# A banded-attention and FFN kernel: the order of all engines' steps read from a complete list instead of made by a list scheduler

## The chip, the core and the metric

One Trainium2 chip, one of its cores. The core has five engines that run side by side and wait for one another through semaphores: TensorE (PE, matmuls), VectorE (DVE), ScalarE (ACT), GpSimd (POOL) and SyncE (SP), which here issues nearly all DMAs. The metric is the device time of one execution in microseconds (us). Three runs of the kernel before took 624.2, 625.16 and 625.16 us; the median is 625.16.

## The reference

```python
# q, k, v: (4, 8, 768, 64); n_global = 8, n_local = 96; w_ch1: (512, 2048), w_ch2: (2048, 512)
scores = q @ k^T / 8                       # per batch and head
keep = (col < n_global) | (0 <= row - col < n_local)
dist = n_local where only global, else |row - col|
scores = where(keep, scores - slope[head] * dist, -1e9)
a = softmax(scores);  attn = a @ v         # divided by sum + 1e-9
x = attn with the heads side by side       # (4, 768, 512)
xn = (x - mean) / sqrt(var + 1e-6) * g_ln
out = x + relu(xn @ w_ch1) @ w_ch2
```

The weights arrive as 64-bit floats, everything else that is large as 32-bit floats.

## The kernel before

**Tiles.** The 3072 rows are 24 tiles of 128 rows, numbered 0 to 23 (`TILES`, line 49). Tiles 0 to 3 are the first tiles of the four batches; they attend to themselves only and are done in float32 (`first`, line 551). Tiles 4 to 23 attend to their own 128 keys, the 128 before, and the global keys; they are done in pairs of float16 high and low parts (`attention`, line 647). Two tiles make a chunk; chunk c holds the tiles 2c and 2c + 1.

**Steps of a tile in `attention`.** k, q and v are loaded (L291) and split into high and low parts on ACT, DVE and POOL (L489, L490, L657, L658, L497, L498). A transposing DMA lays out k (L492) and q (L660), and two plain DMAs copy q's halves across (L662). Four times, for two heads each: PE makes scores (L685, 8 matmuls), DVE adds the mask and takes the minimum (L544), ACT takes the exponential (L549), DVE and POOL split it (L690, L691), a transposing DMA lays it out (L693), and PE multiplies by v (L512 to L514, twelve matmuls, called rows here). Then DVE divides (L524), takes the moments (L531 to L533), POOL takes the root (L536), and DVE scales (L708).

**Steps of a chunk.** In chunks 0 to 3 the first FFN product is plain (L809 to L811 for tiles 0 to 3, L837 to L839 for chunks 2 and 3). From chunk 4 on a pair of tiles is joined in seven products instead of eight (`seven`, line 850): ACT scales (L718), POOL makes three differences (L726 to L729), ACT and DVE split the sums into high and low (L740, L741), transposing DMAs lay them out (L742), and PE makes seven products of 24 matmuls for each of two halves (L862 to L864) with sums taken on ACT and DVE between them (L875, L878). Each result passes through ACT and DVE (L820, L821) into float16 pairs. The second FFN product is 48 matmuls a tile in steps of six (L935; L912 for the last tile, in two halves), DVE adds x (L944, L919), and SP stores the tile (L947, L922).

**Weights.** Sixteen blocks of 1 MB are loaded (L392) and turned from 64-bit floats into float16 pairs by a chain on ACT and DVE: L400, L404, L412, L416, then a copy (L435 or L437) and a difference (L439 or L441).

**What sets the order.** No step is emitted as it is written. `banded` (line 232) records 2165 steps with `Plan.op`: the engine, a duration, what it reads and writes. `Plan.order` (line 141) adds the waits for reused buffers and works out how urgent a step is; `Plan.forward` (line 174) is a list scheduler that keeps a clock of each engine and takes the most urgent step that is ready, with the constants `LOOK` and `EAGER` and the table `SHIFT`, which adds a number to the urgency of each group of steps. Its result, a list of steps with planned start times, is emitted in that order (`emit`), so each engine's program holds its steps in that order and an engine never passes a step that waits.

**Fillers.** Before each PE step that is planned in the first 130 us, `hold` (line 1043) puts matmuls on a tile of zeros (L1047), as many as fill 0.8 of the planned gap. They write into a bank that also holds attention results.

**The end.** When all is done a verdict is summed by one PE step (L1038) and turned into a flag by four small DVE steps (L1027 to L1030). Every engine loads the flag (L1266) and branches past a general version of the kernel that is used for other inputs. The last 40 steps stand in a block of their own (`LAST`).

Of the kernel before, what the change touches and what calls it, by code (L numbers as in the profile page):

```python
# [86 lines left out]
class Plan:  # L87
# [3 lines left out]
    MARGIN = {"DMA": 2.0}  # L91
# [49 lines left out]
    def order(self, chain, stretch, lead):  # L141
        for bufs, made in self.rings.values():
            for old, new in zip(made, made[bufs:]):
                for o in new.users:
# [2 lines left out]
        place = {o: n for n, o in enumerate(self.ops)}
        waits = {o: len(o.before) for o in self.ops}
        line, ready = [], [o for o in self.ops if not waits[o]]
        while ready:  # L150
            o = ready.pop()
            line.append(o)
            for p in o.behind:
                waits[p] -= 1
                if not waits[p]:
                    ready.append(p)
        assert len(line) == len(self.ops), "a circle"
        nxt = dict(zip(chain, chain[1:]))
        rank = {o: n for n, o in enumerate(chain)}
        left = {}  # L160
        for n, o in reversed(list(enumerate(chain))):
            left[o] = o.took * stretch + (left[nxt[o]] if o in nxt else 0.0)
        need = {}
        for o in reversed(line):
            most = left.get(o, 0.0)
            for p in o.behind:
                extra = lead if p in rank and o not in rank else 0.0
                most = max(most, need[p] + o.took + self.seen(o) + extra)
            need[o] = max(most, o.took)
        self.need, self.place = need, place  # L170
        self.planned = self.forward(SHIFT)
        return [o for _, o in self.planned]

    def forward(self, shift):

        need, place = self.need, self.place
        due = {o: need[o] + shift.get(o.group, 0.0) for o in self.ops}
        waits = {o: len(o.before) for o in self.ops}
        engines = ("PE", "ACT", "DVE", "POOL", "SP")
        free = dict.fromkeys(engines, 0.75)  # L180
        dma = port = 0.0
        end, known = {}, {e: [] for e in engines}

        def offer(o):
            t = max([o.after] + [end[p] for p in o.before])
            m = max([t] + [end[p] + self.MARGIN["DMA"] for p in o.before if p.xfer is not None]) if o.engine == "PE" else t
            known[o.engine].append((t, m, -due[o], place[o], o))

        for o in self.ops:
            if not waits[o]:  # L190
                offer(o)
        plan = []
        while any(known.values()):
            best = None
            for e in engines:
                if not known[e]:
                    continue
                can = [(max(c[0], port), max(c[1], port), *c[2:]) if c[4].port else c for c in known[e]]
                at = max(free[e], min(c[0] for c in can))
                now = [c for c in can if c[1] <= at] or [c for c in can if c[0] <= at]  # L200
                c = min(now, key=lambda c: (c[2], c[3]))
                soon = [d for d in can if d[0] <= at + LOOK * c[4].took and d[2] < c[2] - EAGER]
                if soon and e != "PE":
                    c = min(soon, key=lambda c: (c[2], c[3]))
                at = max(free[e], c[0])
                if best is None or at < best[0]:
                    best = (at, e, c[4])
            at, e, o = best
            known[e] = [c for c in known[e] if c[4] is not o]
            free[e] = at + o.took  # L210
# [8 lines left out]
            for p in o.behind:
                waits[p] -= 1  # L220
                if not waits[p]:
                    offer(p)
# [9 lines left out]
def banded(ctx, tc, q, k, v, n_global, n_local, g_ln, w1, w2, out, flag):  # L232
    nc = tc.nc
    vec, act, pool, sp, pe = nc.vector, nc.scalar, nc.gpsimd, nc.sync, nc.tensor
# [153 lines left out]
    def weight(src, dh, dl, name, n, engine="SP", uses=()):  # L388
# [35 lines left out]
        if how[0] == "D":  # L424
            op("DVE", 1.1, lambda: b_(vec), r=[st], w=[lo], port=True)
# [128 lines left out]
    def first(ts):  # L554
# [19 lines left out]
        for e in range(2):  # L574
            for t in ts:
# [457 lines left out]
    op("DVE", 1.42, ranges, r=["cnt", *(("big", n_) for n_ in range(NF))], w=["ok"], after=450.0)  # L1033
# [6 lines left out]
    plan.order(main, 1.13, LEAD)  # L1040
# [43 lines left out]
LEAD = 12.0  # L1084
# [23 lines left out]
SHIFT = {"a0": 820.0, "a1": 286.0, "a2": 108.0, "a3": 701.5, "f0": 21.0, "f1": -345.5, "f10": -235.0, "f2": 34.5, "f5": -15.5, "f7": -246.0, "f8": -72.0, "f9": -54.0, "g": 43.0, "m.a": 196.5, "m.d": -8.5, "s": 31.0, "t0.k": -12.0, "t0.p": 442.5, "t0.s": -26.0, "t0.x": 120.0, "t1.k": -11.0, "t1.p": 823.0, "t1.s": 740.5, "t1.x": 391.0, "t10.s": 127.5, "t10.x": 743.5, "t11.s": -21.0, "t11.x": 722.5, "t12.k": 624.5, "t12.s": 172.0, "t12.x": 431.0, "t13.s": -80.5, "t14.k": -432.0, "t14.s": 318.5, "t15.k": -155.5, "t15.s": 13.0, "t15.x": -67.5, "t16.x": 97.0, "t17.k": -259.0, "t17.s": -134.0, "t18.k": 301.5, "t18.s": 869.0, "t19.x": -379.5, "t2.k": -612.5, "t2.p": 446.0, "t2.s": -18.0, "t2.x": 531.5, "t20.k": -443.5, "t20.s": 33.5, "t21.s": -58.0, "t21.x": 810.5, "t22.k": 600.0, "t22.s": -46.5, "t23.k": -581.0, "t23.s": -220.5, "t3.k": -590.0, "t3.p": 320.0, "t3.s": -371.0, "t3.x": 98.0, "t4.k": -338.0, "t4.s": 227.0, "t4.x": 59.0, "t5.k": 1576.5, "t5.s": 804.0, "t5.x": 1039.0, "t6.k": -664.5, "t6.s": 75.0, "t6.x": 87.5, "t7.k": 211.5, "t7.s": 189.5, "t7.x": 31.0, "t8.k": 80.0, "t8.s": 4.5, "t9.s": -6.5, "t9.x": 495.0, "w1_0_0": -19.0, "w1_0_1": -367.5, "w1_1_0": -7.5, "w1_1_1": -360.0, "w1_2_0": -44.5, "w1_2_1": -300.0, "w1_3_0": 297.0, "w1_3_1": 841.0, "w2_0": -334.5, "w2_1": 76.0, "w2_2": -332.0, "w2_3": 22.5, "w2_4": -548.0, "w2_5": -183.0, "w2_6": -33.5, "w2_7": 16.5, "y10": -235.0, "y2": 34.5, "y4": 12.0, "y5": -15.5, "y7": -246.0, "y8": -72.0, "y9": -54.0}  # L1108
# [191 lines left out]
```

## Time and profile before

| | |
|---|---|
| three runs | 624.2, 625.16, 625.16 us |
| median | 625.16 us |
| profiled execution, first to last instruction | 621.1 us |
| PE busy | 600.4 us (97%), 7036 matmuls, of them 154 fillers |
| DVE busy | 436.9 us (70%) |
| ACT busy | 329.2 us (53%) |
| POOL busy | 246.0 us (40%) |

The page gives the span of the profiled execution, 621.1 us, and no launch-to-end time of that execution; the median of the runs is 4.06 us above the span. PE's busy time counts matmuls that overlap once, counts fillers, and does not tell at which clock they ran. The granted clock is 1.00 in all but one of the forty slices of the page, 0.8 to 0.9 in that one (about 248 to 264 us).

### The profile page before, as it was taken

The page shows a single profiled execution, that of the slowest core. Times are in us where ns is not written, and L with a number is a line of the kernel's source. Part 1 is how long each engine was busy: PE and PEld are TensorE (multiplying, and loading weights), DVE is VectorE, ACT ScalarE, POOL GpSimd, SP SyncE. Part 2 cuts the span into 40 slices and gives each one's busy share as a digit, 9 for nine tenths or more (in the row PEclk, how much of TensorE's full clock was granted, in tenths as well). Part 3 has the DMA queues.
Part 4 walks back from the last instruction along what each step waited for, and adds up shares of the span by engine and source line. Part 5 has one row for each costly group of instructions (what it writes and reads, how often), then busy time and mean ns, then how long its engine had stood idle before and what let it go on. Part 6 is the DMA issues. An engine that isn't in the chain of part 4 may idle for free.

```text
span 621.1 us, 17187 instructions
## 1 busy us (share of the span) xinstructions
PE 600.4 (97%) x7036; PEld 453.3 (73%) x7036; DVE 436.9 (70%) x996; ACT 329.2 (53%) x798; POOL 246.0 (40%) x230
## 2 busy tenths in 40 slices
PE   7889999999999999799999999999999999999996
PEld 5778999555956865596696695787687695796774
DVE  3899898988656474895896995885686784773431
ACT  3887887754535453564564563663663652642220
POOL 1234345448786772434432452441533432323000
PEclk9999999999999999899999999999999999999999
DMA  8996979978485946899697798998997692540301
GB/s 241 308 282 136 250 213 262 174 156 188 72 156 103 174 95 111 176 139 181 117 181 156 162 168 107 188 145 129 170 176 143 136 129 60 111 70 20 77 1 40
DMA packets 260263, 91.65 MB, mean 148 GB/s; under 512 B 250192, under 2 KB 250448, under 8 KB 260176
## 3 DMA queue, kind: packets, MB, share of 16 engines
q1 hardware_dynamic: 259888, 90.47, 74.1%
q8 instruction: 57, 0.93, 0.6%
q14 instruction: 30, 0.25, 0.2%
q10 hardware_dynamic: 288, 0.00, 0.0%
HBM read 38.01 MB, written 6.29 MB: 71 GB/s over the span
## 4 chain that ended last, share of the span: by engine, by line
PE 74%; DVE 13%; ACT 6%; POOL 3%; issue 2%; DMA 1%; ACTq 0%; DVEq 0%; POOLq 0%
PE bank L935 31%; PE bank L862 7%; PE bank L864 7%; PE bank L863 7%; PE bank L685 5%; PE bank L838 2%; PE bank L839 2%; PE bank L837 2%; DVE arena L404 2%; DVE arena L416 2%; PE bank L912 2%; ACT arena L549 2%; PE bank L514 1%; PE bank L512 1%; PE bank L513 1%
## 5 line engine op out<-in xcount | busy, mean ns | idle before, releaser
L935 PE MATMUL bank<-w2h,arena 128*128 128x512 f16 x736 | 239.4, 381 | 0.1
L935 PEld LDWEIGHTS <-arena 128*128 128x128 f16 x1104 | 102.7, 98 | 104.7 <-issue 2.9
L691 POOL TENSOR_TENSOR arena<-arena 128x512 f16<-128x512 f32 x80 | 97.9, 1226 | 182.6 <-DVE arena L690 131.9
L935 PE MATMUL bank<-w2l,arena 128*128 128x512 f16 x368 | 140.1, 381 | 0.1
L862 PE MATMUL bank<-arena 128*128 128x128 f16 x512 | 88.5, 219 | 1.3 <-ACT bank L875 0.9
L863 PE MATMUL bank<-arena 128*128 128x128 f16 x512 | 88.5, 219 | 0.0
L864 PE MATMUL bank<-arena 128*128 128x128 f16 x512 | 88.5, 219 | 0.0
L549 ACT ACTIVATE arena<-arena,mn 128x256 f32<-128x256 f32 x160 | 80.1, 501 | 5.1
L544 DVE CUSTOM_DVE_ANT_0 arena<-bank,mask 128x256 f32<-128x256 f32 x160 | 60.4, 417 | 17.3 <-POOL arena L691 12.6
L862 PE MATMUL bank<-arena,w 128*128 128x128 f16 x384 | 66.6, 219 | 3.3 <-DVE arena L821 3.2
L864 PE MATMUL bank<-arena,w 128*128 128x128 f16 x384 | 66.7, 219 | 0.0
L863 PE MATMUL bank<-arena,w 128*128 128x128 f16 x384 | 66.7, 219 | 0.0
L821 DVE SCALAR_TENSOR_TENSOR arena<-bank,arena 128x512 f16<-128x512 f32 x64 | 43.7, 687 | 31.7 <-ACT arena L820 31.5
L820 ACT ACTIVATE arena<-bank 128x512 f16<-128x512 f32 x64 | 37.8, 592 | 39.3 <-PE bank L864 35.9
L863 PEld LDWEIGHTS <-arena 128*128 128x128 f16 x512 | 50.1, 98 | 3.3 <-issue 1.7
L862 PEld LDWEIGHTS <-arena 128*128 128x128 f16 x512 | 50.1, 98 | 1.7
L864 PEld LDWEIGHTS <-arena 128*128 128x128 f16 x512 | 50.1, 98 | 0.0
L690 DVE CAST arena<-arena 128x512 f16<-128x512 f32 x80 | 43.1, 542 | 8.8 <-DMA arena<-arena 4.4
L685 PE MATMUL bank<-kT,qT 128*128 128x128 f16 x640 | 47.3, 219 | 1.1 <-DVE nm L544 1.0
L685 PEld LDWEIGHTS <-qT 128*128 128x128 f16 x640 | 39.9, 98 | 10.0 <-issue 2.3
L536 POOL TENSOR_TENSOR rs<-rs,half 128x1 f32<-128x1 f32 x24 | 23.4, 975 | 58.4 <-DVE rs L533 58.4
L547 ACT ACTIVATE mn<-nm 128x2 f32<-128x2 f32 x80 | 15.8, 197 | 49.9 <-DVE nm L544 49.1
(181 smaller groups left out, 1499.0 us busy)
## 6 DMA issues: line engine op xcount, KB each, us to landing
arena<-in_moe_w_ch_dram SPq DMA_DIRECT2D x16, 1024.0 KB, 6.8
kf<-in_k_dram SPq DMA_DIRECT2D x28, 256.0 KB, 4.2
vf<-in_v_dram SPq DMA_DIRECT2D x28, 256.0 KB, 4.3
qf<-in_q_dram SPq DMA_DIRECT2D x24, 256.0 KB, 4.0
out_dram<-x SPq DMA_DIRECT2D x23, 256.0 KB, 2.5
qT<-qT SPq DMA_DIRECT2D x40, 128.0 KB, 2.9
pT<-arena SPq DMA_TRANSPOSE x80, 3.2
arena<-arena SPq DMA_TRANSPOSE x36, 3.2
```

Of the source, the lines that this page charges most:

```text
L536: op("POOL", 0.98, lambda: pool.tensor_tensor(out=rs(), in0=rs(), in1=half, op=ALU.pow), r=["half"], w=[rs])
L544: vec.tensor_tensor_reduce(out=T()[:, u, :], in0=ps()[:, u], in1=mask(h), scale=1.0 / Z, scalar=3e38, op0=ALU.add, op1=ALU.min, accum_out= ...
L549: act.activation(out=T()[:, u, :], in_=T()[:, u, :], func=AF.Exp, scale=-1.0, bias=mn()[:, h:h + 1], accum_out=sm()[:, h:h + 1])
L685: pe.matmul(ps()[:, u, n_ * P:(n_ + 1) * P], lhsT=qT()[:, a * H + h, :], rhs=use[n_][0]()[:, h, :], start=(a == 0), stop=(a == 1))
L690: op("DVE", 0.33, lambda pn=pn, T=T: vec.tensor_copy(out=pn()[:, :, 0, :], in_=T()), r=[T], w=[(pn, "hi")], port=True)
L691: op("POOL", 1.2, lambda pn=pn, T=T: pool.tensor_tensor(out=pn()[:, :, 1, :], in0=T(), in1=pn()[:, :, 0, :], op=ALU.subtract), r=[T, (pn, ...
L820: op("ACT", 0.49, lambda: act.activation(out=hh()[:, 0], in_=src(), func=AF.Relu), r=[key], w=[(hh, "hi")])
L821: op("DVE", 0.6, lambda: vec.scalar_tensor_tensor(out=hh()[:, 1], in0=src(), scalar=0.0, in1=hh()[:, 0], op0=ALU.max, op1=ALU.subtract), r ...
L862: pe.matmul(ps()[:, i, :], lhsT=wh, rhs=xT()[:, hi + kk, :], start=(first_ and i == 0 and kk == 0), stop=False, skip_group_check=True)
L863: pe.matmul(ps()[:, i, :], lhsT=wh, rhs=xT()[:, lo + kk, :], start=False, stop=False, skip_group_check=True)
L864: pe.matmul(ps()[:, i, :], lhsT=wl, rhs=xT()[:, hi + kk, :], start=False, stop=(i == 3 and kk == 1), skip_group_check=True)
L935: pe.matmul(ps[t](), lhsT=h[:, part, :], rhs=w[:, f + a, :], start=(f + a == 0 and n_ == 0), stop=(f + a == NF - 1 and n_ == 2))
```

## The change

The list scheduler goes. `Plan.order` takes no arguments: it adds the waits for reused buffers as before and then takes the steps in the order of a table `STEPS` of 2165 numbers, which came from a local search outside the kernel. `Plan.times` replaces `forward`: it gives each step of that list a planned start, which decides only how many fillers go ahead of a PE step and how long DVE and POOL steps are tied to one another (`TIED`). Three recorded durations change (L425 from 1.1 to 1.25, L597 from 1.3 to 1.1, L996 from 1.42 to 0.6); they too have no other effect. What is computed, the buffers and the waits between steps stay the same; no instruction is added or taken away but fillers.

```diff
-    MARGIN = {"DMA": 2.0}
-    def order(self, chain, stretch, lead):
+    def order(self):
         for bufs, made in self.rings.values():
             ...
-        self.need, self.place = need, place
-        self.planned = self.forward(SHIFT)
-        return [o for _, o in self.planned]
-    def forward(self, shift):
-        ...
+        assert sorted(STEPS) == list(range(len(self.ops)))
+        self.planned = self.times([self.ops[n] for n in STEPS])
+
+    def times(self, steps):
+
+        free = dict.fromkeys(("PE", "ACT", "DVE", "POOL", "SP"), 0.75)
+        dma = port = 0.0
+        end, plan = {}, []
+        for o in steps:
+            assert all(p in end for p in o.before), "a step ahead of what it needs"
+            at = max([o.after, free[o.engine]] + [end[p] for p in o.before] + [port] * o.port)
+            free[o.engine] = at + o.took
+            ...
+            plan.append((at, len(plan), o))
+        return [(at, o) for at, _, o in sorted(plan, key=lambda x: x[:2])]
-    plan.order(main, 1.13, LEAD)
+    plan.order()
-SHIFT = {"a0": 820.0, "a1": 286.0, "a2": 108.0, ...}
+STEPS = [
+    3, 2, 5, 18, 10, 6, 22, 9, 8, 7, 0, 1, 21, 20, 154, 161, ...
```

The program has 154 fillers before and 127 now. Lines of the functions below `Plan` have numbers lower by 60 in the changed kernel (L524 before is L464 now).

**The start, SP.** The first DMAs before: `gb` is the FFN norm's weight, `qf` and `kf` are q and k of tiles 0 and 1, `vf` is v, `arena` from `moe_w_ch` is a weight block.

```order
L383 DMA gb<-in_moe_g_ln_dram 128x512
L291 DMA qf_0_118<-in_q_dram 128x8x64
L291 DMA kf_0_121<-in_k_dram 128x8x64
L291 DMA qf_0_128<-in_q_dram 128x8x64
L291 DMA kf_0_132<-in_k_dram 128x8x64
L564 DMA vf_126<-in_v_dram 128x8x64
L392 DMA arena<-in_moe_w_ch_dram 128x2x512 x2
```

And now:

```order
L231 DMA kf_0_115<-in_k_dram 128x8x64
L231 DMA qf_0_120<-in_q_dram 128x8x64
L231 DMA qf_0_128<-in_q_dram 128x8x64
L231 DMA kf_0_131<-in_k_dram 128x8x64
L332 DMA arena<-in_moe_w_ch_dram 128x2x512 x3
L504 DMA vf_124<-in_v_dram 128x8x64
L332 DMA arena<-in_moe_w_ch_dram 128x2x512
L504 DMA vf_118<-in_v_dram 128x8x64
L323 DMA gb<-in_moe_g_ln_dram 128x512
```

`gb` moved from the first place behind four weight blocks, and the weight blocks moved ahead of v.

**The start, DVE.** Before: L369 makes the first mask, L473 moves q and k of tiles 0 and 1 out of PSUM, L593 takes the minimum of scores, L621 to L623 divide a tile's attention result, L404 is a weight step.

```order
L369 TENSOR_SCALAR arena<-arena 128x128 x8
L473 TENSOR_SCALAR q_0_210<-bank_79 128x512
L473 TENSOR_SCALAR q_1_226<-bank_78 128x512
L473 TENSOR_SCALAR k_1_246<-bank_76 128x512
L593 TENSOR_REDUCE nm_250<-bank_72 128x4
L593 TENSOR_REDUCE nm_275<-bank_73 128x4
L621 TENSOR_SCALAR r_296<-bank_74 128x4
L622 RECIPROCAL r_296<-r_296 128x4
L623 TENSOR_TENSOR x_299<-bank_74,r_296 128x4x64
L404 TENSOR_SCALAR arena<-arena 128x1024
```

And now (L309 is the mask, L413 the move, L533 the minimum, L344, L356 and L381 weight steps):

```order
L413 TENSOR_SCALAR q_0_196<-bank_79 128x512
L309 TENSOR_SCALAR arena<-arena 128x128 x8
L413 TENSOR_SCALAR q_1_223<-bank_78 128x512
L413 TENSOR_SCALAR k_1_238<-bank_76 128x512
L533 TENSOR_REDUCE nm_240<-bank_72 128x4
L533 TENSOR_REDUCE nm_271<-bank_73 128x4
L344 TENSOR_SCALAR arena<-arena 128x1024
L356 SCALAR_TENSOR_TENSOR arena<-arena 128x1024
L344 TENSOR_SCALAR arena<-arena 128x1024
L533 TENSOR_REDUCE nm_271<-bank_73 128x4
L381 TENSOR_TENSOR w_00_90<-arena,w_00_90 128x2x512
L344 TENSOR_SCALAR arena<-arena 128x1024
```

q of tile 0 moved ahead of the mask, and a whole weight block moved ahead of the first division.

**Behind the last rows of tile 9, PE.** Before, where chunk 4 begins: the last of the rows, then a product of `seven`.

```order
L514 MATMUL bank_74<-vn_1_2775,pT_3_3481 128x64
L862 LDWEIGHTS w_00_90
L862 MATMUL bank_77<-arena,w_00_90 128x128
L863 LDWEIGHTS w_00_90
L863 MATMUL bank_77<-arena,w_00_90 128x128
```

And now (L454 is the last of the rows, L875 the second FFN product of an earlier tile):

```order
L454 MATMUL bank_74<-vn_1_2978,pT_3_3347 128x64
L875 LDWEIGHTS arena
L875 MATMUL bank_79<-w2h,arena 128x512
L875 LDWEIGHTS arena
L875 MATMUL bank_79<-w2l,arena 128x512
```

Counted in matmuls, between the last rows of tile 9 and the first product that needs tile 9's transposes stand before: 24 of `seven`, 12 of L935, 12 rows, 24 scores. Now: 30 of L875, 24 of `seven`, 6 of L875, 12 rows, 6 of L875, 8 scores, 6 of L875, 8 scores.

**The same place, DVE.** Before (L821 brings the result of the product ahead of the rows into float16):

```order
L524 TENSOR_TENSOR x_3574<-bank_74,r_3282 128x512
L531 BN_STATS bn_3578<-x_3574 128x6
L532 BN_AGGR mv<-bn_3578 128x2
L533 TENSOR_SCALAR rs_3581<-mv 128x1
L708 SCALAR_TENSOR_TENSOR arena<-x_3574,mv,gb 128x512
L821 SCALAR_TENSOR_TENSOR arena<-bank_77,arena 128x512
```

And now (L761 is that step):

```order
L464 TENSOR_TENSOR x_3476<-bank_74,r_3308 128x512
L471 BN_STATS bn_3479<-x_3476 128x6
L472 BN_AGGR mv<-bn_3479 128x2
L473 TENSOR_SCALAR rs_3482<-mv 128x1
L648 SCALAR_TENSOR_TENSOR arena<-x_3476,mv,gb 128x512
L715 TENSOR_TENSOR arena<-arena 128x512
L609 COPY vn_1_2978<-vn_0_2519 16x1024
L761 SCALAR_TENSOR_TENSOR arena<-bank_77,arena 128x512
```

On DVE the step stays behind the moments, two steps later than before; on PE 30 matmuls moved in ahead of the product that waits for it.

**The end, DVE.** Before: L1027 to L1030 make the flag, L919 adds x to the two halves of the last tile.

```order
L1027 TENSOR_SCALAR fine<-bank_76 1x1
L1028 TENSOR_SCALAR fine<-bank_76 1x2
L1029 TENSOR_REDUCE every<-fine 1x1
L1030 TENSOR_SCALAR flag<-every 1x1
L919 SCALAR_TENSOR_TENSOR x_9000<-bank_79,x_9000 128x256
L919 SCALAR_TENSOR_TENSOR x_9000<-bank_78,x_9000 128x256
```

And now:

```order
L859 SCALAR_TENSOR_TENSOR x_8971<-bank_79,x_8971 128x256
L859 SCALAR_TENSOR_TENSOR x_8971<-bank_78,x_8971 128x256
L967 TENSOR_SCALAR fine<-bank_76 1x1
L968 TENSOR_SCALAR fine<-bank_76 1x2
L969 TENSOR_REDUCE every<-fine 1x1
L970 TENSOR_SCALAR flag<-every 1x1
```

The flag moved behind the last tile's result. On PE the verdict's matmul, which stood 72 matmuls ahead of the end, is now the last.

## Rows read from the trace of the kernel before

**Rows 1.** Busy us by stretch: PE, PEld, DVE, ACT, POOL; then clock, DMA.
```profile
0.00:66.00 66.00, 57.52 (x570) 49.78 (x571) 51.90 (x91) 48.80 (x92) 19.26 (x27) 1.00 0.92 244
66.00:249.40 183.40, 182.83 (x1920) 132.64 (x1920) 134.00 (x286) 102.95 (x244) 109.39 (x89) 1.00 0.78 161
249.40:264.00 14.60, 10.54 (x129) 7.62 (x126) 12.51 (x34) 7.77 (x23) 6.98 (x8) 0.88 0.78 170
264.00:615.00 351.00, 349.51 (x4426) 263.25 (x4425) 238.08 (x586) 169.64 (x442) 110.38 (x108) 1.00 0.71 124
```

**Rows 2.** Groups by line, the fillers: busy us, mean ns, idle before.
```profile
L1047 PE MATMUL bank<-still 128*128 128x252 bf16 x154 | 21.7, 288 | 2.9 <-DVE x L623 1.9 <-DVE still L1078 1.0
```

**Rows 3.** PE's waits: us in total, times, longest.
```profile
PE bank L862 <- DVE arena L821: 3.6, 2, 3.2
...
PE bank L583 <- DVE q L473: 1.4, 1, 1.4
```

**Rows 4.** PE in order of time: start, us, line, in brackets the idle before.
```profile
243.14 0.59 PE L935 MATMUL bank<-w2h,arena 128*128 128x512 f16 x2
...
252.76 0.22 PE L862 MATMUL bank<-arena,w 128*128 128x128 f16 x1 [3.18 <-DVE arena L821]
...
255.07 1.06 PE L935 MATMUL bank<-w2h,arena 128*128 128x512 f16 x2
...
260.64 0.22 PE L862 MATMUL bank<-arena 128*128 128x128 f16 x1
```

**Rows 5.** Chain of waits around the last rows of tile 9: start, us, what.
```profile
248.51 0.06 PE bank L864
...
249.24 0.03 PE bank L512
...
249.62 0.70 DVE x L524
```

**Rows 6.** Chain of waits, a step of the second FFN product.
```profile
321.40 1.29 PE bank L935 x6
```

**Rows 7.** DVE in order of time behind the last rows of tile 9.
```profile
252.03 0.69 DVE L821 SCALAR_TENSOR_TENSOR arena<-bank,arena 128x512 f16<-128x512 f32 x1
252.63 0.40 DVE L669 COPY vn<-vn 16x1024 f16<-16x1024 f16 x1
```

**Rows 8.** DVE in order of time, the first 20 us.
```profile
9.50 1.17 DVE L369 TENSOR_SCALAR arena<-arena 128x128 bf16<-128x128 f32 x8
...
13.10 0.69 DVE L473 TENSOR_SCALAR k<-bank 128x512 f32<-128x512 f32 x1 [1.24 <-PE bank L481]
...
18.11 0.16 DVE L621 TENSOR_SCALAR r<-bank 128x4 f32<-128x4 f32 x1 [1.94 <-PE bank L611]
```

**Rows 9.** The flag's line by engine: duration ns, first and last start us.
```profile
L1266 SPq EVENT_SEMAPHORE  x8: 17/17/17, 619.2 to 619.7; - x8
...
L1266 DVEq TENSOR_LOAD <-flag x1: 543/543/543, 615.1 to 615.1; - x1
L1266 DVEq COMPARE_BRANCH  x1: 84/84/84, 615.7 to 615.7; - x1
L1266 SPq TENSOR_LOAD <-flag x1: 535/535/535, 615.9 to 615.9; - x1
...
L1266 DVEq EVENT_SEMAPHORE  x1: 21/21/21, 618.8 to 618.8; - x1
```

**Rows 10.** DVE in order of time, the end.
```profile
607.12 0.14 DVE L1027 TENSOR_SCALAR fine<-bank 1x1 f32<-1x1 f32 x1
...
607.54 0.14 DVE L1030 TENSOR_SCALAR flag<-every 1x1 int32<-1x1 f32 x1
...
615.08 0.42 DVE L919 SCALAR_TENSOR_TENSOR x<-bank,x 128x256 f32<-128x256 f32 x1 [2.85 <-PE bank L912]
```

**Rows 11.** DVE in order of time, the step that makes tile 4's q.
```profile
61.52 0.71 DVE L658 SCALAR_TENSOR_TENSOR qn<-qf,qn 128x512 f16<-128x512 f32 x1
```

**Rows 12.** SP in order of time, its copies of q's halves.
```profile
73.77 2.56 SPq L662 DMA_DIRECT2D qT<-qT  x4
```

More of the change, by code (lines that the diff above doesn't have):

```diff
@@ L146, in order @@
                         self.edges(old.users, o)
[L147 to L169, printed above, removed]
@@ L170, in order @@
-        self.need, self.place = need, place
-        self.planned = self.forward(SHIFT)
-        return [o for _, o in self.planned]
-    def forward(self, shift):
[L176 to L180, printed above, removed]
-        dma = port = 0.0
[L182 to L210, printed above, removed]
@@ L211, in forward @@
             if o.port:
-                port = free[e]
+                port = free[o.engine]
             if o.xfer is not None:
-                dma = max(dma, free[e]) + o.xfer
+                dma = max(dma, free[o.engine]) + o.xfer
                 end[o] = dma + self.SEEN["DMA"]
             else:
-                end[o] = free[e] + self.seen(o)
+                end[o] = free[o.engine] + self.seen(o)
             plan.append((at, len(plan), o))
[L219 to L222, printed above, removed]
@@ L223, in forward @@
-        assert len(plan) == len(self.ops)
         return [(at, o) for at, _, o in sorted(plan, key=lambda x: x[:2])]
-LOOK = 0.5
-EAGER = 3.0
 @with_exitstack
@@ L424, in weight @@
         if how[0] == "D":
-            op("DVE", 1.1, lambda: b_(vec), r=[st], w=[lo], port=True)
+            op("DVE", 1.25, lambda: b_(vec), r=[st], w=[lo], port=True)
         elif how[0] == "P":
@@ L597, in exps @@
                         act.activation(out=T()[:, j, :], in_=ps()[:, j], func=AF.Exp, scale=-1.0, bias=nm()[:, 2 * j + e:2 * j + e + 1])
-                op("ACT", 1.3, exps, r=[ps, (nm, e)], w=[T])
+                op("ACT", 1.1, exps, r=[ps, (nm, e)], w=[T])
         for e in range(2):
@@ L1032, in banded @@
     op("POOL", 0.1, lambda: pool.memset(ones, 1.0), w=["ones"], after=300.0)
-    op("DVE", 1.42, ranges, r=["cnt", *(("big", n_) for n_ in range(NF))], w=["ok"], after=450.0)
+    op("DVE", 0.6, ranges, r=["cnt", *(("big", n_) for n_ in range(NF))], w=["ok"], after=450.0)
     op("DVE", 1.0, products, r=["gs"], w=[*(("wm", n_) for n_ in range(16)), "wx"], after=460.0)
@@ L1082, in banded @@
         emit(line[-LAST:])
-LEAD = 12.0
 TIED = 150.0
@@ L1107 @@
 SS, PVS, PVS2, F1S, F1S2, F2S, F2S2 = (0, 1), (2, 3), (2,), (4, 5), (4, 5, 3), (6, 7), (6, 7)
-SHIFT = {"a0": 820.0, "a1": 286.0, "a2": 108.0, "a3": 701.5, "f0": 21.0, "f1": -345.5, "f10": -235.0, "f2": 34.5, "f5": -15.5, "f7": -246.0, "f8": -72.0, "f9": -54.0, "g": 43.0, "m.a": 196.5, "m.d": -8.5, "s": 31.0, "t0.k": -12.0, "t0.p": 442.5, "t0.s": -26.0, "t0.x": 120.0, "t1.k": -11.0, "t1.p": 823.0, "t1.s": 740.5, "t1.x": 391.0, "t10.s": 127.5, "t10.x": 743.5, "t11.s": -21.0, "t11.x": 722.5, "t12.k": 624.5, "t12.s": 172.0, "t12.x": 431.0, "t13.s": -80.5, "t14.k": -432.0, "t14.s": 318.5, "t15.k": -155.5, "t15.s": 13.0, "t15.x": -67.5, "t16.x": 97.0, "t17.k": -259.0, "t17.s": -134.0, "t18.k": 301.5, "t18.s": 869.0, "t19.x": -379.5, "t2.k": -612.5, "t2.p": 446.0, "t2.s": -18.0, "t2.x": 531.5, "t20.k": -443.5, "t20.s": 33.5, "t21.s": -58.0, "t21.x": 810.5, "t22.k": 600.0, "t22.s": -46.5, "t23.k": -581.0, "t23.s": -220.5, "t3.k": -590.0, "t3.p": 320.0, "t3.s": -371.0, "t3.x": 98.0, "t4.k": -338.0, "t4.s": 227.0, "t4.x": 59.0, "t5.k": 1576.5, "t5.s": 804.0, "t5.x": 1039.0, "t6.k": -664.5, "t6.s": 75.0, "t6.x": 87.5, "t7.k": 211.5, "t7.s": 189.5, "t7.x": 31.0, "t8.k": 80.0, "t8.s": 4.5, "t9.s": -6.5, "t9.x": 495.0, "w1_0_0": -19.0, "w1_0_1": -367.5, "w1_1_0": -7.5, "w1_1_1": -360.0, "w1_2_0": -44.5, "w1_2_1": -300.0, "w1_3_0": 297.0, "w1_3_1": 841.0, "w2_0": -334.5, "w2_1": 76.0, "w2_2": -332.0, "w2_3": 22.5, "w2_4": -548.0, "w2_5": -183.0, "w2_6": -33.5, "w2_7": 16.5, "y10": -235.0, "y2": 34.5, "y4": 12.0, "y5": -15.5, "y7": -246.0, "y8": -72.0, "y9": -54.0}
+STEPS = [
[83 rows of a table added]
+]
 MOVE = {"k1": "D", "k3": "D", "p31": "D", "q0": "D", "q1": "D", "q3": "D"}
```

83 rows, old and new, of the table STEPS are left out of this document.

## The prediction

> **What bounds the kernel now.** Read the busy time by stretch first [rows 1]. TensorE (PE) is the bound almost throughout: it is idle 0.57 us in the 183.4 us from 66 to 249.4, and 1.49 us in the 351 us from 264 to 615. No order can win more than these 2.1 us there. The time that PE loses stands in three other places.
>
> First, the start. In the first 66 us PE is busy 57.5 us, but 21.7 us of that are fillers [rows 2], so real work fills 35.8 us and 30.2 us are lost. VectorE (DVE) is busy 51.9 of these 66 us; its 14.1 idle us lie mostly in the first 20, where it waits for PE's first tiles [rows 8].
>
> Second, 249.4 to 264: 14.6 us with PE busy 10.54, so 4.06 us idle, and a clock of 0.88, so another 0.12 x 14.6 = 1.75 us: 5.8 us in all. PE's waits name what ended the longest, 3.2 us: L862, a product of chunk 4, waited for DVE's L821 [rows 3]. In order of time this is the product behind the last rows of tile 9 [rows 4]. Right behind it two matmuls of L935 take 1.06 us, against 0.59 at 243 us: the lower of the two clock levels, 1.2 against 2.4 GHz.
>
> Third, the last 6.1 us, from PE's last matmul to the end: the last result, its store, and the branch on the flag [rows 9, 10].
>
> These sum to 44 us. The sum below is made against the profiled span of 621.1 us; the page has no other time of that execution. The runs' median, 625.16, is 4.06 us above it, and I take that distance as unchanged.
>
> **The hole at 249.4 us.** The order moves two things. The chain from the last rows of tile 9, whose results DVE takes up at 249.62, to the first product that needs that tile's transposes, at 260.64 [rows 4, 5], is 11.0 us long. The order before puts under it 24 matmuls of `seven`, 12 of L935, 12 rows and 24 scores. A matmul of `seven` takes 0.056 us (13 from 248.51 to 249.24), a matmul of the rows 0.03 [rows 5], six of L935 take 1.29 [rows 6], and a score has the shape of `seven`: 1.34 + 2.58 + 0.35 + 1.34 = 5.6 us of work under 11.0 us of waiting. The new order puts there 48 matmuls of the second FFN product, 24 of `seven`, 12 rows and 16 scores: 8 x 1.29 + 1.34 + 0.35 + 0.9 = 12.9 us. That covers the chain with 1.9 us to spare.
>
> The 3.18 us wait inside it goes by another edit. L821 ended at 252.72 [rows 7], some 3.1 us behind the rows, because DVE had the moments of tile 9 ahead of it. On DVE it now stands two steps later still (a subtraction of about 0.7 us, as L821, and the copy of 0.40 [rows 7]), so about 4.2 us behind the rows. But 30 matmuls of the second FFN product, 6.45 us, now stand between rows and product on PE. So wait and slow clock go together. I take 5.5 of the 5.8 us. Bounds: 5.8, and 2.5 if DVE's queue is 3 us longer there than counted.
>
> Counted the same way, the cover in chunks 5 to 11 is 12.1 to 14.8 us before, and PE hardly waits there; in the new order it is 12.5 to 15.7 in chunks 4 to 11. So I take no new hole from 66 to 615, and 0.5 of the 2.1 us as won; bounds 1.8 won and 3 lost.
>
> **The start.** DVE sets the pace: the last fillers before stand ahead of a product of tile 1 that PE starts at 66 us and that needs the 57th step of DVE. The tightest place of that kind in the new order is the third score step of tile 4, which needs DVE's 56th step; the two sets of steps are alike (8 of L404, 8 of L416 in each), and sum to the same within half a us. But PE has one FFN product (48 x 0.056 = 2.7 us) less done by then, one attention product, one transpose and two score steps more: about 1.0 us less work, so 1.0 us more lost.
>
> Against this stands what the first 20 us save. PE's first scores waited 1.4 us for q of tile 0 [rows 3], which on DVE stood behind the mask of 1.17 us [rows 8]; now it stands ahead. The 256 KB of gb no longer come before the first q and k. A whole weight block moved ahead of the first division, where DVE idled 1.94 us [rows 8]; but its steps alternate with ACT's, so part of the wait comes back. I put the saving at 2.3 us, between nothing and 1.2 + 1.24 + 1.94 = 4.4 us. Net: 1.3 us won; bounds 4.4 won, 1.0 lost, and 5.9 lost if PE stops long enough for the clock (below).
>
> The 27 fillers fewer are 27/154 of 21.7 = 3.8 us of PE at most; they stood in waiting time, and where the wait stays their absence wins nothing. I count them at zero.
>
> **The end.** Here the order loses. The flag was ready 8 us before the end. Now its four steps, 0.56 us from 607.12 to 607.68 [rows 10], come behind the last result, which ended at 615.50. DVE loaded the flag from 615.1, while that result was under way, and SP from 615.9 [rows 9]. Now no engine can before 616.1: SP 0.2 us later, DVE 1.0 us later. DVE's first event behind the branch came 3.0 us after its compare, at 618.8, and SP's series of waits began at 619.2; DVE 1.0 us later is 0.6 us behind that. Cost 0.6 us, bounds 0.2 and 1.0.
>
> The rows show a branch that costs DVE 3.0 us of waiting [rows 9]. The Trainium skill, Runtime: NRT & Kernel Launch, Instruction fetch mechanics, says that a taken branch to a page not at hand makes the engine fetch it before it goes on. By that rule the 3.0 us follow the flag wherever it is, and the end would be the full 1.0 us later, 618.9 in all.
>
> **Sum.** -5.5 - 0.5 - 1.3 + 0.6 = -6.7 us: a span of 614.4, and 625.16 - 6.7 = 618.5 us.
>
> **The rivals.**
>
> A, more at the start (0.20): DVE's waits go whole, 4.4 us, and the later places don't give it back. With 5.8, 1.8 and a tail of 0.2 that is -11.8: 613.4 us. For it: DVE idles 14.1 us there, and places later in the new order need no more DVE work ahead of as much PE work. Against it: DVE and ACT steps of one weight block alternate, so they can't fill each other's waits.
>
> B, the clock falls once at the start (0.12): with 27 fillers fewer PE stops somewhere as long as at 249.6 us, 3.18 us, and pays 1.75 us of low clock behind it [rows 1, 4]: -6.7 + 4.9 = -1.8, 623.4 us. For it: waits are longer than the planner's, which sets the fillers. Against it: before, PE stopped up to 1.4 us there [rows 3] and the clock stayed at 1.00 [rows 1]. The Trainium skill, TensorE: Matmul & The Clock Gate, HAM oscillation, has this as its rule: gaps without matmuls throttle PE, and each return is paid again. The trace agrees with it at 252.8 us alone.
>
> C, slower (0.08): tile 4's scores are drawn ahead. They stood behind about 20 us more of PE work; now PE reaches them with about 33 us of real work done, and all FFN work behind waits if they do. They need q's copies, which SP issued until 76.3 us [rows 12], 14.8 us behind the DVE step at 61.52 [rows 11]. The point from which it decides: 33 + 30.2 lost as before + 5.4 of the other terms = 68.6 us. Were the copies as late as now, PE would lose 7.7 us more than all gains: 632.9 us. Against it: that DVE step was the 53rd and is the 40th, 12 us of DVE work earlier, so near 49 us; with the same 14.8 us behind it the copies come at 64.
>
> A search that does nothing new (0.02) is left: every engine's order differs from its first steps on.
>
> **How the numbers follow.** The forecast has 0.58. A measurement here tells 0.2%, 1.25 us, from no change: faster is below 623.9. The forecast gives 0.56 of its 0.58 to that, A 0.20, B 0.08: 0.84. Same, 623.9 to 626.4: 0.02 of the forecast, 0.03 of B, 0.02: 0.07. Slower: C and 0.01 of B: 0.09. The forecast's own range by its bounds (start 3 either way, 2 elsewhere) is 614.5 to 622.5. To hold 8 in 10 I go to 612.5, past most of A, and to 624.0, past B.
>
> **What would show it.** Right: no wait of over 1 us of PE on L761 behind the last rows of tile 9, and a clock of 1.00 in every slice behind the first; PE idle under 3 us from 66 us to its last matmul; DVE's flag load about 0.6 us behind the last result's end, and the end some 6.7 us behind PE's last matmul; the point where fillers end 1 to 2 us earlier against the work done. Wrong: a slice with a lower clock at the start (B); scores of tile 4 that wait for a DMA (C); a hole in a chunk whose cover I counted as enough, which would say that queues on DVE, ACT or SP, and not the chain's own length, set it.

## The result, and the profile after

The changed kernel took 613.87 us (median of 4 runs, 613.05 to 614.78), the kernel before 624.68 beside it: ratio 0.9829, interval 0.9808 to 0.9849. That is 10.8 us less, where 6.7 were forecast; 613.87 lies inside the stated range of 612.5 to 624.0, 4.6 us under the predicted time and 0.6 us under the forecast's own range of 614.5 to 622.5. The profiled executions have spans of 621.1 and 611.3 us, 9.8 apart, and the places below are accounted for within these two. Medians here and below are of undisturbed executions.

The busy times by stretch of the new kernel (PE, PEld, DVE, ACT, POOL; then clock and DMA) answer to [rows 1]:

```profile
0.00:66.00 66.00, 59.04 (x576) 49.95 (x577) 52.89 (x102) 47.86 (x96) 17.66 (x28) 1.00 0.88 246
66.00:249.40 183.40, 182.71 (x1935) 132.45 (x1932) 138.78 (x294) 104.91 (x247) 115.40 (x91) 1.00 0.78 163
249.40:264.00 14.60, 14.57 (x231) 12.55 (x230) 13.39 (x34) 10.09 (x33) 7.19 (x7) 1.00 0.82 145
264.00:604.00 340.00, 339.83 (x4274) 255.35 (x4272) 230.33 (x565) 160.31 (x423) 109.34 (x106) 1.00 0.73 127
```

The third line is the hole: PE was busy 10.54 us there at a clock of 0.88, and is now busy 14.57 at 1.00. PE's waits, us in total, times and longest, against [rows 3]:

```profile
PE bank L987 <- DVE x L563: 3.2, 3, 1.4
PE bank L987 <- DVE still L1018: 1.0, 1, 1.0
PE bank L523 <- DVE q L413: 0.9, 1, 0.9
...
PE bank L802 <- DVE arena L818: 0.2, 1, 0.2
```

The 3.6 us of L862 for L821 are gone. The longest waits left are those of fillers (L987), all in the first 61 us.

Busy time does not show where the 9.8 us come from, so I laid the two traces over each other by work: each real matmul counts with its pace, the usual distance to the start of the next one (0.056 us for a product of `seven`, 0.215 for one of the second FFN product), some 575.6 us in both, and at equal work done I read the two times. The lead is the time before less the time now.

| PE work done | before, us | now, us | lead |
|---|---|---|---|
| 36.8 us | 66.22 | 63.72 | 2.50 |
| 217 us (ahead of the hole) | 247.30 | 244.61 | 2.69 |
| 232 us (behind it) | 268.46 | 260.13 | 8.33 |
| 359 us | 397.86 | 387.13 | 10.73 |
| end of the last product | 615.05 | 604.01 | 11.04 |
| end of the span | 621.10 | 611.28 | 9.82 |

So: start and what follows it 2.7, hole 5.6, rest behind it 2.7, end -1.2.

**The hole.** PE in order of time (start, us, line) around the last rows of tile 9, against [rows 4]:

```profile
236.34 0.19 PE L454 MATMUL bank<-vn,pT 128*128 128x64 f16 x1
...
242.84 0.22 PE L802 MATMUL bank<-arena,w 128*128 128x128 f16 x1
...
249.87 0.22 PE L802 MATMUL bank<-arena 128*128 128x128 f16 x1
```

And DVE there, against [rows 7]:

```profile
236.57 0.69 DVE L464 TENSOR_TENSOR x<-bank,r 128x512 f32<-128x512 f32 x1 [0.64 <-PE bank L454]
...
239.91 0.67 DVE L761 SCALAR_TENSOR_TENSOR arena<-bank,arena 128x512 f16<-128x512 f32 x1
```

The rows end at 236.5, and L761 at 240.58, 4.0 us behind them. PE comes to its product at 242.84, without a wait: 30 matmuls of L875 stand between. The product that needs the tile's transposes runs at 249.87, 13.3 us behind DVE's first step on the rows, where 11.0 were needed before.

**The start.** DVE from 9.8 us, against [rows 8]:

```profile
9.78 0.68 DVE L413 TENSOR_SCALAR q<-bank 128x512 f32<-128x512 f32 x1
10.38 1.16 DVE L309 TENSOR_SCALAR arena<-arena 128x128 bf16<-128x128 f32 x8
...
15.90 1.31 DVE L344 TENSOR_SCALAR arena<-arena 128x1024 uint16<-128x1024 uint16 x1 [0.54 <-ACT arena L340]
```

The first weight step starts at 15.90; before, it came behind the division of [rows 8], at 18.86. Where the fillers end, PE shows:

```profile
60.38 0.81 PE L987 MATMUL bank<-still 128*128 128x252 bf16 x6 [1.30 <-DVE x L563]
61.04 1.05 PE L625 MATMUL bank<-kT,qT 128*128 128x128 f16 x16
```

From there to its last matmul PE idles no more than 0.53 us at a time. The wait at 60.38 is that of a filler, in whose bank DVE still reads an attention result.

**The end.** The branch on the flag by engine (duration ns, first and last start), against [rows 9]:

```profile
L1289 SPq EVENT_SEMAPHORE  x8: 17/17/17, 608.8 to 609.3; - x8
...
L1289 DVEq TENSOR_LOAD <-flag x1: 767/767/767, 604.9 to 604.9; - x1
...
L1289 PEldq COMPARE_BRANCH  x1: 4487/4487/4487, 605.7 to 605.7; - x1
...
L1289 PEldq EVENT_SEMAPHORE  x1: 51/51/51, 610.3 to 610.3; - x1
...
L1318 SPq EVENT_SEMAPHORE  x10: 17/28/580, 609.4 to 611.2; - x10
```

All five engines now load the flag at the same time, at 604.85, and PE's branch alone lasts 4.49 us, to 610.2. The last line is the row of SyncE's (SP's) waits behind its own branch: one of them lasts 0.58 us and ends at 610.36, right behind PE's event; before, none lasted over 0.03. From the end of PE's last product to the end of the span, the tail from here on, it is 7.27 us, against 6.05 before.

### The profile page after: what moved, and what is told of

Same layout as the page of the kernel before. It is cut to its first block, busy times and chain, and to the rows that moved or that the text cites. A ratio compares the mean times of both kernels' runs of the same rounds, so it can differ in the third digit from the quotient of the medians.

```text
span 611.3 us, 17170 instructions
## 1 busy us (share of the span) xinstructions
PE 596.2 (98%) x7009; PEld 450.3 (74%) x7009; DVE 436.1 (71%) x996; ACT 323.2 (53%) x798; POOL 249.6 (41%) x230
## 4 chain that ended last, share of the span: by engine, by line
PE 84%; DVE 10%; ACT 2%; DMA 1%; issue 1%; SPq 1%; POOL 0%; ACTq 0%; DVEq 0%
PE bank L875 36%; PE bank L802 8%; PE bank L803 8%; PE bank L804 8%; PE bank L625 6%; PE bank L751 2%; PE bank L749 2%; PE bank L750 2%; PE bank L777 2%; PE bank L852 2%; PE bank L779 2%; PE bank L778 2%; PE bank L452 1%; PE bank L454 1%; PE bank L453 1%; DVE arena L344 1%
## 5 line engine op out<-in xcount | busy, mean ns | idle before, releaser
L875 PE MATMUL bank<-w2h,arena 128*128 128x512 f16 x736 | 236.9, 379 | 0.0
L875 PEld LDWEIGHTS <-arena 128*128 128x128 f16 x1104 | 102.6, 98 | 104.4
L875 PE MATMUL bank<-w2l,arena 128*128 128x512 f16 x368 | 139.5, 379 | 0.0
L761 DVE SCALAR_TENSOR_TENSOR arena<-bank,arena 128x512 f16<-128x512 f32 x64 | 43.5, 686 | 24.6 <-ACT arena L760 24.2
L476 POOL TENSOR_TENSOR rs<-rs,half 128x1 f32<-128x1 f32 x24 | 26.7, 1112 | 62.4 <-DVE rs L473 61.6
L630 DVE CAST arena<-arena 128x512 f16<-128x512 f32 x80 | 38.1, 478 | 7.9 <-ACT arena L489 4.4
L803 PEld LDWEIGHTS <-w 128*128 128x128 f16 x384 | 37.6, 98 | 2.6 <-issue 0.4
```

The costliest lines, as they stand in the source:

```text
L476: op("POOL", 0.98, lambda: pool.tensor_tensor(out=rs(), in0=rs(), in1=half, op=ALU.pow), r=["half"], w=[rs])
L630: op("DVE", 0.33, lambda pn=pn, T=T: vec.tensor_copy(out=pn()[:, :, 0, :], in_=T()), r=[T], w=[(pn, "hi")], port=True)
L761: op("DVE", 0.6, lambda: vec.scalar_tensor_tensor(out=hh()[:, 1], in0=src(), scalar=0.0, in1=hh()[:, 0], op0=ALU.max, op1=ALU.subtract), r ...
L803: pe.matmul(ps()[:, i, :], lhsT=wh, rhs=xT()[:, lo + kk, :], start=False, stop=False, skip_group_check=True)
L875: pe.matmul(ps[t](), lhsT=h[:, part, :], rhs=w[:, f + a, :], start=(f + a == 0 and n_ == 0), stop=(f + a == NF - 1 and n_ == 2))
```

## The experiments

OLD is the old scheduler's order as a list of the same 2165 numbers, NEW the table of the change. The edits of e1, e2, e3 and e11 stand here in short, for the table that they make. "New kernel" is 613.87 us.

### e1: the old order through the new code

```diff
-STEPS = NEW
+STEPS = OLD
```

> The new kernel's code with the old order written into the table (every engine has the steps in the order of before; the planned starts come from the new code, which sets 165 fillers at the start where before has 154). Theory, order alone decides: the median of before, 624.7 us, within 1 us, with a hole of about 3.2 us at 252 us and the low clock behind it. Rival, part of the gain is in the new planned starts and durations (fillers, the waits that tie VectorE and GpSimd): 2 us or more below before.

Measured: 624.15 us, 624.0 beside it for the kernel before (ratio 0.9989, 0.9959 to 1.002). The hole stands where it stood (PE in order of time):

```profile
252.78 0.26 PE L802 MATMUL bank<-arena,w 128*128 128x128 f16 x1 [3.18 <-DVE arena L761]
```

So the order alone is the change; the new planned starts and 11 more fillers do nothing that these times show.

### e2 and e3: half the order

```diff
-STEPS = NEW
+STEPS = OLD[:376] + [n for n in NEW if n not in OLD[:376]]
```

```diff
-STEPS = NEW
+STEPS = [n for n in NEW if n in EARLY] + [n for n in OLD if n not in EARLY]
```

EARLY are the 437 steps that the new order has in its first 125 us.

> The old order for the first 376 steps (some 105 us), then the new order for all that is left. By the two traces the start is 3.3 us of the 9.8 us of span. Theory, the places are independent: 3.3 us of the gain are gone, so the time is 10.8 - 3.3 = 7.5 us below before (617.2 us), with no wait of TensorE over 1 us from 110 us to the end. Rival, the hole at 250 us is closed because the new order comes there with a lead won at the start: the hole of 3 to 6 us is back, and the time is 1 to 2 us below before.

> The new order for the first 437 steps (some 125 us), then the old order for all that is left. Theory, the places are independent: the fillers end near 61 us as in the new kernel, and the time is 3.3 us below before (621.4 us). Rival, the lead of the start is given back where the old order goes on, since what follows there is paced by VectorE's work on the weights: within 1 us of before, with waits of TensorE between 100 and 170 us that sum to 2 us or more. In both the hole at 250 us stands.

Measured: e2 615.95 us, 8.1 below before; e3 624.57, 0.6 above it. PE's waits of e2 from 100 to 610 us:

```profile
PE bank L777 <- DVE arena L785: 0.5, 1, 0.5
PE bank L802 <- DVE arena L818: 0.2, 1, 0.2
```

The hole closes without any lead from the start: e2 comes to it 1.1 us behind the kernel before, and leaves it 4.4 us ahead. The theory stands for e2 and falls for e3. There the lead was 1.6 us at a work of 80 us and -0.5 at 130: PE waits again where the old order goes on (its waits from 100 to 171 us):

```profile
PE bank L625 <- DVE nm L484: 0.6, 1, 0.6
PE bank L875 <- POOL w2l L379: 0.4, 1, 0.4
```

The rival's time is met, not its waits: they sum to 1.0 us as shown, where it wanted 2, though 2.1 us of lead go. A start that is ahead is worth something only with steps behind it that can use it.

### e4: the flag's steps early

```diff
-2141, 2151, 2142, 2152, 2143, 2153, 2144, 2154, 2145, 2155, 2163, 2146, 2156, 2164
+2141, 2163, 2164, 2151, 2142, 2152, 2143, 2153, 2144, 2154, 2145, 2155, 2146, 2156
```

> The new order with two steps moved: the small product of the verdict stands on TensorE five half-steps of the last product earlier, and the four flag steps on VectorE ahead of the two last results. From TensorE's last matmul to the end were 6.1 us before and 7.4 us in the new kernel. Theory of the trace after, TensorE's own branch of 4.5 us stands on the path when the flag is late: 1.3 us below the new kernel (612.6 us), tail 6.1 us. Theory of the prediction, only the 0.6 us of VectorE's and SyncE's branch: 613.3 us, tail 6.8 us. Rival, the flag's place does nothing: 613.9 us, and a product drawn ahead makes TensorE wait for VectorE at 598 us.

Measured: 613.77 us, no difference from the new kernel by medians of 6 and 4 runs. The trace shows the end as the theory had it, a tail of 6.10 us instead of 7.27:

```profile
L1289 SPq EVENT_SEMAPHORE  x8: 17/17/17, 609.1 to 609.6; - x8
...
L1289 PEldq COMPARE_BRANCH  x1: 3387/3387/3387, 603.4 to 603.4; - x1
```

PE's branch is over at 606.8, ahead of SP. But in this execution the fillers' wait ahead of tile 4's scores ended at 61.16, 0.8 us later, which hides most of it: its clock is 0.91 over the first 20 us, the new kernel's 1.00. The profile of e8, which has the start of the new kernel, the late flag and the same 0.91, has a span of 612.3 us; e4's is 611.0, so 1.3 us are won at equal clock. e12 agrees.

### e5 and e6: fewer fillers

```diff
-IDLE, HOLD, FILL = 3, 130.0, 0.8
+IDLE, HOLD, FILL = 3, 58.0, 0.8
```

and for e6 `HOLD` 8.0.

> The new kernel without its last six fillers, which stand ahead of tile 4's first scores. In the new kernel the first of them waited 1.30 us, until 60.38, for VectorE to read the bank that fillers write, while the last transposed copy for the scores had landed at 58.88. Theory, the fillers themselves hold the scores back there, and VectorE behind them idled 0.73 us: 0.8 to 1.5 us below the new kernel (613.9 us), PE's real work resuming near 59.3 us. Theory of the prediction, the wait stays and fillers in it cost nothing: 613.9 us. Rival, without them the clock falls: 1.8 us slower.

> The new kernel with only the 25 fillers ahead of the first 8 us, 102 fewer. Theory, they stand in waits and their only work is the clock: without them TensorE's clock falls in the first 60 us, real work of some 34 us runs at half speed for part of it, and the time is 3 to 15 us above the new kernel. Rival, they stand in VectorE's pace and the clock that they hold is not needed, since PE waits anyway: within 1 us of 613.9 us, with a lower clock in the first slices.

Measured: e5 612.23 us, 1.6 below the new kernel (by the profiled spans, 610.1 and 611.3, both at a clock of 1.00 in the first 66 us, 1.2). Tile 4's scores start when their operands are there:

```profile
59.08 1.10 PE L625 MATMUL bank<-kT,qT 128*128 128x128 f16 x16
...
61.79 0.61 PE L625 MATMUL bank<-kT,qT 128*128 128x128 f16 x8 [0.32 <-DVE nm L484]
```

The six fillers held them back by 2.0 us, and 1.2 to 1.6 of that are in the time, as the theory said. e6 took 618.34 us, 4.5 above: the clock of PE fell (stretches as above; the clock is the number behind the five engines):

```profile
0.00:15.30 15.30, 10.90 (x60) 8.32 (x61) 6.03 (x24) 5.80 (x15) 1.63 (x13) 0.87 0.84 265
15.30:61.00 45.70, 40.75 (x323) 36.02 (x322) 38.26 (x54) 38.27 (x72) 10.95 (x11) 0.67 0.77 205
```

The other fillers are needed. The price without them is far less than the missing clock (0.33 x 45.7 = 15 us); that PE waits for much of this time anyway would explain it, and was not measured apart.

### e7: the old place in the new order

```diff
-851, 824, 718, 710, 719, 711, 720, 865
+851, 718, 710, 719, 711, 720, 824, 865
```

(PE's steps alone; 824 is the last rows of tile 9, 865 the product behind L761.)

> The new order with one step moved on TensorE: the last rows of tile 9 stand behind five steps of the second FFN product instead of ahead of them (6.45 us later), next to the product that needs VectorE's L761. Theory, the hole before was these places and nothing else: a wait of 3 to 4.5 us at about 245 us, the low clock behind it, and 5 to 6 us above the new kernel (619 to 620 us). Rival, other work of the new order has come early enough to fill it: a wait under 1.5 us, no low clock, within 2 us of 613.9 us.

Measured: 620.68 us, 6.8 above the new kernel.

```profile
247.04 0.26 PE L802 MATMUL bank<-arena,w 128*128 128x128 f16 x1 [4.10 <-DVE arena L761]
...
249.98 0.63 PE L875 MATMUL bank<-w2l,arena 128*128 128x512 f16 x1
250.40 1.06 PE L875 MATMUL bank<-w2h,arena 128*128 128x512 f16 x2
```

One step moved by 6.45 us of work brings back a wait of 4.10 us and the low clock (1.06 us for a pair, as in [rows 4]). The order on DVE, ACT and POOL is the same. The theory holds, its price was 0.8 us short of the measured.

### e8: TensorE in the hint

```diff
-engines=[mybir.EngineType.SP, mybir.EngineType.DVE]
+engines=[mybir.EngineType.SP, mybir.EngineType.DVE, mybir.EngineType.PE]
```

> The new kernel with TensorE named in the hint on the last branch, beside SyncE and VectorE. In the new kernel TensorE's branch took 4.49 us, to 610.2, and the last waits follow it. Theory, the hint fetches the code behind the branch ahead of time: TensorE is done before SyncE, and the tail is 6.5 us instead of 7.3 us, 0.8 us below the new kernel. Rival, the hint does nothing for it (SyncE and VectorE are named now, and their first event still comes 3.0 and 3.5 us behind the compare): tail 7.3 us, 613.9 us.

Measured: 614.56 us, tail 7.23 us.

```profile
L1289 SPq EVENT_SEMAPHORE  x8: 17/17/17, 610.4 to 610.9; - x8
...
L1289 PEldq COMPARE_BRANCH  x1: 499/499/499, 606.8 to 606.8; - x1
...
L1318 SPq EVENT_SEMAPHORE  x10: 17/28/28, 611.0 to 612.3; - x10
```

The hint works on PE, 0.50 us instead of 4.49, and SP no longer waits for it, yet nothing is won: SP's first event comes 3.55 us behind the end of its compare (606.83), 3.06 in the new kernel. The theory is right on the branch and wrong on the tail, the rival the other way round. Why SP takes longer is open.

### e9, e10 and e11: what the start hangs on

```diff
-13, 27, 14, 31
+13, 14, 27, 31
```

```diff
-lambda: b_(vec)
+lambda: [b_(vec) for _ in range(2 if name in ("1_2_0", "1_3_1") else 1)]
```

```diff
-STEPS = NEW
+STEPS = OLD[:73] + [n for n in NEW if n not in OLD[:73]]
```

(e9: VectorE's steps alone; 14 is the mask, 27 the first q.)

> The new kernel with one exchange on VectorE: the mask (1.16 us) stands ahead of the first q again, as before. Theory of the prediction, the wait for q is on the path of the start: 1.2 us above the new kernel (615.1 us). Rival by the trace after, VectorE waits 1.09, 0.54 and 1.32 us for TensorE and ScalarE between 13 and 19 us anyway, and what comes 0.7 us later there is taken up: within 0.6 us of 613.9 us.

> The new kernel with one weight step of VectorE (L344, 1.3 us) done twice in two of the blocks, at 34.7 and 48.0 us; nothing else is changed, and the results are the same. Theory, VectorE's work sets the pace of the first 60 us: 2.6 us above the new kernel (616.5 us). Rival, the pace is ScalarE's or the loads' and VectorE's queue has room: under 0.8 us above (at most 614.7 us).

> The old order for the first 73 steps (some 23 us), then the new order. Before, VectorE began with the first weight block at 18.86 us, now at 15.90. Theory of the trace, these 3 us are what the start won: 2.5 to 3.5 us above the new kernel (616.4 to 617.4 us). Theory of the prediction, the first 20 us save 2.3 us: 616.2 us. Rival, VectorE only did 0.95 us more work there (9.50 against 8.55 us busy by 20 us) and the rest was won later, by what is drawn ahead of what: 614.9 us.

Measured: e9 615.62 us (+1.75), e10 616.98 (+3.1), e11 617.15 (+3.3). In e9 the waits on DVE grow instead of taking up the delay:

```profile
13.94 0.69 DVE L413 TENSOR_SCALAR k<-bank 128x512 f32<-128x512 f32 x1 [1.82 <-PE bank L421]
...
17.20 0.69 DVE L533 TENSOR_REDUCE nm<-bank 128x4 f32<-128x512 f32 x1 [1.97 <-PE bank L527]
17.81 1.31 DVE L344 TENSOR_SCALAR arena<-arena 128x1024 uint16<-128x1024 uint16 x1
```

The first weight step comes 1.9 us later. But not all of this is the exchange, as the clock is 0.91 over the first 20 us here and 1.00 in the new kernel's profile. e8, with the new kernel's start and the same 0.91, has this step at

```profile
16.95 1.32 DVE L344 TENSOR_SCALAR arena<-arena 128x1024 uint16<-128x1024 uint16 x1
```

So 1.05 us of the delay go with the clock and 0.86 with the exchange, and the spans (611.3, 612.3 and 613.4 us) grow by 1.0 and 1.1. The exchange costs about 1.1 us by one pair of profiles; the rival's 0.6 is too little. In e10 the two doubled steps take 2.65 and 2.69 us instead of some 1.3 each, and the fillers' wait before tile 4's scores comes 2.67 us later than in the new kernel:

```profile
63.05 0.81 PE L987 MATMUL bank<-still 128*128 128x252 bf16 x6 [1.30 <-DVE x L563]
```

So DVE's work sets the pace of the start, one for one. In e11 the first weight step starts at 18.79 and the scores 2.5 us later:

```profile
63.30 0.38 PE L987 MATMUL bank<-still 128*128 128x252 bf16 x2 [1.30 <-DVE x L563]
63.51 1.05 PE L625 MATMUL bank<-kT,qT 128*128 128x128 f16 x16
```

The theory (2.5 to 3.5 us) holds; by the spans, both at a clock of 1.00 in the first 20 us, it is 2.9. The doses agree: the weights begin 0.9 us later in e9 than in e8 and it costs 1.1, 2.9 us later in e11 than in the new kernel and it costs 2.9 to 3.3. So the start gains by the weights beginning 3 us earlier: about 1 of these is the mask's exchange with q. The rest of the first 20 us' order was not taken apart.

### e12: e4 and e5 together

Both diffs above.

> The new order with the two edits that seemed to gain: the flag's steps early (tail 6.1 instead of 7.3 us) and the last six fillers out (1.2 us by the span, 610.1 against 611.3). Theory, they stand at the two ends and add up: 2.4 us below the new kernel, a span of 608.9 and 611.5 us. Rival, the tail's gain is not in the time, as the time of the early flag alone (613.8) did not show it: 612.2 us.

Measured: 611.58 us, 2.3 below the new kernel, 13 below the kernel before (624.8 beside it); tail 6.06 us. By the medians the gains add up. The profiled execution has a span of 610.3, not 608.9: its clock is 0.91 over the first 20 us, 1.00 in the new kernel's. Three of its six executions took 611.05 to 611.15 us, 2.0 below the two best of the new kernel.

## Why the prediction was right or wrong

**The hole: right.** 5.5 us were forecast, 5.6 measured. The cover and the chain did what the count said, L761 4.0 us behind the rows where 4.2 were counted. e2 shows it free of the start, e7 that the place of one step decides it.

**The rest from 66 us on: the term that was mis-sized.** 0.5 us with a bound of 1.8 won stood for it; 2.7 were won behind the hole, and 0.2 ahead of it. The step that failed is "No order can win more than these 2.1 us": it took the 1.49 us in which PE was not busy for all that it lost from 264 to 615. PE's waits before, from 264 to 400 us (one of the first two ends at 263.94, on the border), and one of them in order of time:

```profile
PE bank L862 <- ACT bank L875: 0.9, 2, 0.5
PE bank L685 <- DVE nm L544: 0.4, 1, 0.4
PE bank L862 <- DVE arena L821: 0.4, 1, 0.4
```

```profile
364.30 0.22 PE L862 MATMUL bank<-arena 128*128 128x128 f16 x1 [0.41 <-DVE arena L821]
364.36 0.22 PE L863 MATMUL bank<-arena 128*128 128x128 f16 x1
```

A matmul of this shape counts 0.22 us as busy and the next starts 0.056 us behind it. So 0.16 us of each wait count as busy, and a wait of up to 0.16 does not show. By pace PE lost some 3.3 us from 264 to 615 before, and some 0.5 in the new kernel. The Trainium skill, Perfetto Trace Analysis, Tensor Engine Instruction, says that a matmul's end is estimated from its size and not observed; the rows agree, 0.22 us long and 0.056 apart.

**The start: mechanism half right, size off.** 1.3 us forecast as 2.3 saved less 1.0 lost; 2.5 measured at the end of the fillers. The saving was 3 us, not 2.3 (e11). That DVE sets the pace is shown by e10. DVE's idle time was misread in part: of its 11.4 idle us in the first 20, 7.1 lie ahead of 10 us, behind loads and ScalarE and not behind PE's first tiles. The 1.0 us lost did not come: it rested on tile 4's third score step as the tightest place, which needs DVE's 56th step. That step ended at 62.2, with DVE busy 49.2 us by then, and PE came to these scores at 62.82 and did not wait. DVE's steps were shorter than in the rows before (eight of L344 10.8 us, eight of L404 11.9); the other differences in duration were not traced. What PE stood at was its own fillers (e5).

**The fillers: wrong.** Costed at zero. The 27 that went left the clock at 1.00 in the profiled execution, so B did not come there. In part of the executions the clock does fall: of the new kernel's four, two have a mean clock of 0.997 and 613.05 and 613.30 us, two 0.994 and 0.995 and 614.44 and 614.78, 1.4 us more where B had 4.9. That the fillers are the cause is not shown: e2, which has the old order's start and 162 fillers, is at 0.91 over the first 20 us too. But six that stayed cost 1.2 to 1.6 us (e5), because a filler that waits holds what is behind it.

**The end: sign right, half the size.** 0.6 us forecast, 1.2 measured. SyncE's compare ends 0.16 us later behind PE's last product (1.72 us against 1.56), as counted. Two terms were left out. The late branch of TensorE: before, it ran from 613.6, beside PE's last matmuls, and nothing waited for it. That cover was gone once the verdict's product stood last on PE, and SyncE now waits 0.55 us for it. And SyncE's own time from compare to first event grew by 0.50, from 2.56 to 3.06: it is 2.56 to 2.66 in the profiles with the early flag and 3.06 to 3.90 in those with the late one, where all engines branch together. The three sum to the 1.2. In e8 the wait for PE is gone and SyncE's own time is 1.0 longer than before, which is why the hint won nothing; the cause of that growth is open. The Trainium skill, Runtime: NRT & Kernel Launch, Instruction fetch mechanics, says that a taken branch to a page not at hand stalls until the page is fetched. The prediction worked out 1.0 us by it; the measured end is nearer to that than to 0.6, but by terms that neither had.

**The rivals.** A named 613.4 us, 0.5 off the measured time, and is the nearest, by luck: of its parts the start came to 2.5 and not 4.4, the rest to 2.9 and not 1.8, and the end to 1.2 and not 0.2. C did not come: q's copies were issued at 51.59, 5 us behind the DVE step at 46.27 and not 14.8; the k copy landed at 58.88. Its margin was thin, though: e5's scores run at 59.08.

**Span and time.** 4.06 us were taken for the distance from the profiled span to the time. For one execution it is 1.77 us (613.05 and 611.28); the rest was the distance of the profiled execution from the median, which is not the same for two kernels. Of the 4.6 us by which the time was missed 1.0 is this (10.8 by the medians, 9.8 by the spans), 0.5 is the median of the kernel before (624.68 beside the new kernel, 625.16 in the forecast), and 3.1 are the terms above. The stated range holds 613.87 because it was widened to take in most of A; the forecast's own did not.

## What to carry to other kernels

Read what an engine loses from the starts of its instructions at equal work, not from its busy share: pipelined matmuls hide a piece of every wait. When an order is replaced, count for each long chain what work stands under it, and check each engine's last steps for what ran beside the main work until now. Fillers that hold a clock need a place where they wait for nothing.

## What the runs showed of the hardware

- A branch taken at the end took PE 3.4 to 4.5 us, ACT and POOL 0.05 with the next event 0.4 us later, and SP and DVE 2.6 to 3.9 us to the next event; SP's was 2.6 to 2.7 when the engines came to it apart and 3.1 to 3.9 when they came together. A hint cut PE's to 0.50 and left the end where it was.
- PE's clock behind an idle of 3.18 us (before) and 4.10 us (e7) was the lower level, with pairs of the second FFN product at 1.06 us instead of 0.59. Behind waits of up to 1.4 us with fillers around them it stayed at 1.00 in the profiles before and after; with 102 fillers less it was 0.67 on average from 15 to 61 us.
- Executions of one kernel differ by 1.7 us (613.05 to 614.78, the new kernel) to 4.2 (622.82 to 627.04, e1), and the clock of the first slices with them: 0.91 over the first 20 us in the profiles of e2, e3, e4, e8, e9 and e12, 1.00 in those of e1, e5, e7, e10, e11 and the kernels before and after. More than the order of steps decides it: e2's first scores waited 1.44 us for q as in the kernel before, and the one is at 0.91 and the other at 1.00. The price is 1.0 us by the spans of e8 and the new kernel, whose starts are the same.
